# One transformer block, forward and backward: W1 and dW1 in blocks of two steps, with another order of pools and of the middle phase

## The chip, the cores and the metric

The kernel runs on one core of a Trainium2 chip. The metric is the time of one execution on the device, in microseconds (us). A core has a matrix engine (TensorE, PE in the profile), a vector engine (VectorE, DVE), a scalar engine (ScalarE, ACT), a general engine (GpSimd, POOL) and a queue engine that here only issues transfers (SyncE, SP). Each of them works through its own instructions in order. Transfers are issued from SP and from POOL and are carried out by 16 DMA engines. SBUF is the working memory with 128 partitions; PSUM holds the sums of matmuls.

## The reference

The kernel computes one block with adaptive layer norm, and all its gradients. Cut to its core:

```python
mod = (silu(c) @ w_mod).reshape(1, 6, 1, 512)       # sa, ca, ga, sb, cb, gb
h = layernorm(x) * (1 + ca) + sa
x = x + ga * attention(h, wqkv, wo)                 # 2048 tokens, 32 heads of 16, softmax
h = layernorm(x) * (1 + cb) + sb
u = h @ w1 + b1                                     # 512 -> 1792
x = x + gb * (relu(u) ** 2 @ w2 + b2)               # 1792 -> 512
# outputs: x, and the gradients of x, wqkv, wo, w1, b1, w2, b2, c, w_mod for a given grad_out
```

Inputs and outputs are bf16. For the change it matters that du, the gradient of u, is computed from grad_out; that dW1 is a product of the normalised x (xhat2) and du over all tokens, with two corrections that also need W1; and that dW2 is a product of relu(u)**2 and grad_out.

## The kernel before

The work is written out in one order, in the class `K`. `phase_fwd` runs forward attention head pair by head pair over four chunks of 512 tokens (`SC` = 4) and, between its steps, the qkv projections and the MLP with the first half of its backward part (`gen_mlp`) for chunks 0 to 2. `last_chunk` then does the MLP of chunk 3, for which there is no attention left to lie beside, and the weight gradients of the MLP. `phase5` is attention backward over 8 groups of four heads (`NQ`), two head pairs each, and `phase6` computes the rest. The order of TensorE and of SP is the program's own throughout; from attention backward on, POOL's is too. The order on VectorE and ScalarE (and on POOL before attention backward) is set by a planner, which keeps to program order where it can. Semaphores are set by the framework from what each tile is read and written by.

**The middle phase, `last_chunk`.** `bg` is what is left of chunk 2's MLP, `bg.take(n)` takes n units of it. For each of four blocks of 128 tokens the attention output is turned (`turn`, four transposes and a copy) and multiplied by wo (L800); x is added (L801), the layer norm's numbers are computed on VectorE and POOL (L802 to L806), and ScalarE writes the normalised block `xh` (L807). `xh` is turned to `xhT`. fc1 (L821) makes 14 tiles of relu(u) in `rT`; du (L794, the helper `du_mm`, which reads `gT`, the turned grad_out) makes 14 tiles that VectorE combines with `rT` to `duT` (L828). Three of the du tiles, `early[0]` to `early[2]`, are computed ahead: two inside the loop over blocks and one between the turns of `xh`; they lie in the PSUM pool `dps`, which has three banks. Then follow, for block k: `dx(k)` (L848, and the layer norm backward), `fc2(k)` (L879), `turn_dx(k)`, `do(k)` (L1237: the gradient of the attention output, its row sums, and the padded tile `dOpad`), and `turn_do(k)` (dOpad turned into `dOTq`, stored from SP by L874 after every second k). The order is written by hand:

```python
        fc2(2)
        turn_dx(2)
        fc2(3)
        turn_do(1)
        do(2)
```

**dW1 and dW2.** `fill` holds two generators. `gen_dw1` works in 14 steps of 128 columns of W1 (`FT`): 64 matmuls (L964) of `xh2` with the turned du block `du_blk` (a transposing load from `duT_d` on SP, L944, three buffers, issued two steps ahead), one small matmul with `diag` (L969), and then on ScalarE and VectorE the dW1 block and two dot products with the W1 block. One step has 16 units for `fill.take`. POOL loads the W1 block of each step (L947, three buffers of 128 columns), computes `diag` (L949) and stores the dW1 block (L985, two buffers). A block of 128 columns in bf16 is a run of 256 B in a row of W1 in memory. `gen_dw2` works in 14 steps of 16 matmuls (L1015) with `a_blk` (four buffers), then multiplies on VectorE (L1018), stores from POOL (L1019), and adds to a sum on POOL (L1022). The last such step is the last work ahead of attention backward.

**Pools.** SBUF is handed out as a stack from the left and one from the right. In the middle phase the left one holds, from below, e0 (x1, grad_out, xhat2), dw1 and dw2. They are closed at the end of `last_chunk`; `phase5` opens p56a (the gradients of q, k and v), p5pu (the exponentials `pu`, six buffers), p5kv, p5dt (`dsT`, four) and p5ds (`ds`, three), in this order, in the same place. A tile whose memory was held by a closed pool waits for those who used it.

**Attention backward.** For each head pair, each chunk of 512 keys and each group of four blocks of 128 queries: scores on TensorE (L1497), exponential on ScalarE (L1501), dP on TensorE (L1436), ds on VectorE (L1438), the key and value gradients (L1390), ds turned (a quarter by TensorE, L1455, copied by ScalarE, L1456; the rest by a transposing transfer on SP, L1446), and the query gradient (L1412). There are 256 such groups; each has eight exponentials and eight ds.

Of the kernel before, what the change touches and what calls it, by code (L numbers as in the profile page):

```python
# [9 lines left out]
BF16 = mybir.dt.bfloat16  # L10
F32 = mybir.dt.float32
# [8 lines left out]
P = 128  # L20
# [85 lines left out]
class K:  # L106
# [636 lines left out]
    def last_chunk(self, bg, O_b, x0s):  # L743
# [42 lines left out]
        ve = mk.tile([P, 4], F32, name="ve")  # L786
        rstd = mk.tile([P, 4], F32, name="rstd2")
        nmr = mk.tile([P, 4], F32, name="nmr")
        early = {}

        def du_mm(ft, pool, name):
            pt = pool.tile([P, 512], F32, name=name)
            for kt in range(DT):
                nc.tensor.matmul(pt[:], lhsT=self.W2gbT[:, ft, kt, :], rhs=gT[:, kt, :], start=(kt == 0), stop=(kt == DT - 1))  # L794
            return pt

        for k in range(4):
            pt = mps.tile([P, 512], F32, name="pps")
            for kt in range(DT):
                nc.tensor.matmul(pt[:], lhsT=OT[:, k, kt, :], rhs=self.wo[:, kt, :], start=(kt == 0), stop=(kt == DT - 1))  # L800
            nc.vector.tensor_tensor(x1[:, k, :], pt[:], x0s[k][:], ALU.add)  # L801
            nc.vector.bn_stats(stats[:, k, :], x1[:, k, :])  # L802
            nc.vector.bn_aggr(mv[:, k, :], stats[:, k, :])
            nc.vector.tensor_scalar(ve[:, k:k + 1], mv[:, k, 1:2], EPS, None, ALU.add)
            nc.gpsimd.tensor_tensor(rstd[:, k:k + 1], ve[:, k:k + 1], self.mhalf[:, k:k + 1], ALU.pow)
            nc.vector.scalar_tensor_tensor(nmr[:, k:k + 1], mv[:, k, 0:1], -1.0, rstd[:, k:k + 1], ALU.mult, ALU.mult)  # L806
            nc.scalar.activation(xh[:, k, :], x1[:, k, :], ACT.Identity, bias=nmr[:, k:k + 1], scale=rstd[:, k:k + 1])  # L807
            bg.take(1)
            if k > 1:
                early[k - 2] = du_mm(k - 2, self.dps, "dps")  # L810
        bg.drain()
        xhT = mk.tile([P, 4, DT, P], BF16, name="fT", bufs=2)
        for k in range(4):
            turn(xh[:, k, :], DT, xhT[:, k], "vector" if k % 2 else "scalar")
            if k == 2:
                early[2] = du_mm(2, self.dps, "dps")
        rT = self.rT_pool.tile([P, FT, 512], BF16, name="rT")
        for ft in range(FT):
            pt = mps.tile([P, 512], F32, name="pps")
# [4 lines left out]
        self.close_pool("mlp_u")  # L824
        duT = mk.tile([P, FT, 512], BF16, name="auT")
        for ft in range(FT):
            pt = early.get(ft) or du_mm(ft, mps, "pps")
            nc.vector.scalar_tensor_tensor(duT[:, ft, :], pt[:], 2.0, rT[:, ft, :], ALU.mult, ALU.mult,  # L828
                                           accum_out=self.db1_part[:, ft, sc:sc + 1])
            nc.scalar.activation(rT[:, ft, :], rT[:, ft, :], ACT.Square)  # L830
# [27 lines left out]
        def turn_dx(k):  # L858
            dxT = mk.tile([P, DT, P], BF16, name="dxT", bufs=2)
            turn(dxTs[k], DT, dxT[:], "scalar")  # L860
            dxTs[k] = dxT
# [5 lines left out]
        def turn_do(k):  # L867
            if k % 2 == 0:
                self.dOTq = mk.tile([P, NQ, 2 * P], BF16, name="dOTq")
            c0 = k % 2 * P  # L870
            turn(dOpads[k][:].rearrange("p g j e -> p (g j e)"), NQ, self.dOTq[:, :, c0:c0 + P], "scalar")
            if k % 2:
                t0 = (st0 + k - 1) * P
                nc.sync.dma_start(self.dOTq_d.rearrange("g p s -> p g s")[:, :, t0:t0 + 2 * P], self.dOTq[:])  # L874
# [20 lines left out]
        do(1)  # L895
        fc2(2)
        turn_dx(2)
        fc2(3)
        turn_do(1)
        do(2)  # L900
        self.close_pool("mlp_f")
        w2p = self.open_pool("dw2", bufs=2)
        g2 = self.gen_dw2(w2p, g_tm)
        fill.add(g2)
        fill.take(8)
        turn_dx(3)
        fill.take(8)
        turn_do(2)
        do(3)
        fill.take(24)  # L910
        turn_do(3)
        for name in ("mlp0", "mlpk"):
            self.close_pool(name)
# [13 lines left out]
    def gen_dw1(self, sb, xh2):  # L927
        nc, io = self.nc, self.io
        D, F, ST, DT, FT = self.D, self.F, self.ST, self.DT, self.FT
        db1 = self.db1  # L930
        w1_v = io["B_w1"].rearrange("(kt p) f -> p kt f", p=P)
        dw1_v = io["out_4"].rearrange("(kt p) f -> p kt f", p=P)
        dcb_part = sb.tile([P, DT, FT], F32, name="dcb_part", bufs=1)
        dsb_part = sb.tile([P, DT, FT], F32, name="dsb_part", bufs=1)
        db1_row = sb.tile([1, F], BF16, name="db1_row", bufs=1)
        nc.vector.memset(dcb_part[:], 0.0)
        nc.vector.memset(dsb_part[:], 0.0)
        blks = []

        def load(ft):  # L940
            r = sb.tile([P, ST, P], BF16, name="du_blk", bufs=3)
            cuts = (0, ST - 4, ST) if ft < 2 else (0, ST)
            for (a, b) in zip(cuts, cuts[1:]):
                nc.sync.dma_start_transpose(r[:, a:b, :], self.duT_d[ft, :, a * P:b * P])  # L944
            w = sb.tile([P, DT, P], BF16, name="w1_blk", bufs=3)
            with nc.allow_non_contiguous_dma(reason="256B runs"):
                nc.gpsimd.dma_start(w[:], w1_v[:, :, ft * P:(ft + 1) * P])  # L947
            diag = sb.tile([P, P], F32, name="diag", bufs=3)
            nc.gpsimd.tensor_scalar(diag[:], self.ident_f[:], db1[:, ft:ft + 1], 1.0, ALU.mult, ALU.mult)  # L949
            blks.append((r, w, diag))  # L950

        for ft in range(2):
            load(ft)
        yield 0
        for ft in range(FT):
            if ft + 2 < FT:
                load(ft + 2)
            else:
                yield ("dw1", 0)
            du, w1_blk, diag = blks[ft]  # L960
            g4 = self.dps.tile([P, DT, P], F32, name="dps")
            for kt in range(DT):
                for st in range(ST):
                    nc.tensor.matmul(g4[:, kt, :], lhsT=xh2[:, st, kt * P:(kt + 1) * P], rhs=du[:, st, :],  # L964
                                     start=(st == 0), stop=(st == ST - 1))
                    if st % 4 == 3:
                        yield 1
            csb_ps = self.mps.tile([P, 512], F32, name="pps")
            nc.tensor.matmul(csb_ps[:, :P], lhsT=self.ones_f[:], rhs=diag[:], start=True, stop=True)  # L969
            csb = sb.tile([P, P], F32, name="csb")  # L970
            nc.scalar.copy(csb[:], csb_ps[:, :P])
            nc.scalar.copy(db1_row[:, ft * P:(ft + 1) * P], csb_ps[0:1, :P])
            t1 = sb.tile([P, DT, P], F32, name="t1")
            dw1 = sb.tile([P, DT, P], BF16, name="dw1")
            for kt in range(DT):
                nc.scalar.activation(t1[:, kt, :], csb[:], ACT.Copy, scale=self.mod_col(3)[:, kt:kt + 1])
                nc.vector.scalar_tensor_tensor(dw1[:, kt, :], g4[:, kt, :], self.opcbT[:, kt:kt + 1], t1[:, kt, :], ALU.mult, ALU.add)
                junk = sb.tile([P, P], F32, name="junk")
                nc.vector.scalar_tensor_tensor(junk[:], g4[:, kt, :], 1.0, w1_blk[:, kt, :], ALU.mult, ALU.mult,
                                               accum_out=dcb_part[:, kt, ft:ft + 1])  # L980
                junk2 = sb.tile([P, P], F32, name="junk")
                nc.vector.scalar_tensor_tensor(junk2[:], csb[:], 1.0, w1_blk[:, kt, :], ALU.mult, ALU.mult,
                                               accum_out=dsb_part[:, kt, ft:ft + 1])
            with nc.allow_non_contiguous_dma(reason="256B runs"):
                nc.gpsimd.dma_start(dw1_v[:, :, ft * P:(ft + 1) * P], dw1[:])  # L985
        nc.gpsimd.dma_start(io["out_5"].rearrange("(o f) -> o f", o=1), db1_row[:])
        nc.vector.tensor_reduce(self.dcb_col[:], dcb_part[:], axis=AX.X, op=ALU.add)
        nc.vector.tensor_reduce(self.dsb_col[:], dsb_part[:], axis=AX.X, op=ALU.add)
# [286 lines left out]
    def phase5(self):  # L1275
        S, D, NQ, ST, DT = self.S, self.D, self.NQ, self.ST, self.DT
        nc, io = self.nc, self.io
        opa = self.open_pool("p56a", bufs=1)
        self.pup = self.open_pool("p5pu", bufs=6)
        self.dq_t = opa.tile([P, ST, D], BF16, name="dq_t")  # L1280
        self.dk_t = opa.tile([P, ST, D], BF16, name="dk_t")
# [8 lines left out]
        self.parts = [self.dq_t, self.dk_t, self.dv_t]  # L1290
        self.stp = self.open_pool("p5st", bufs=3, space=PSUM)
        self.dpp = self.open_pool("p5dp", bufs=3, space=PSUM)
        self.kvp = self.open_pool("p5kv", bufs=1)
        self.dtp = self.open_pool("p5dt", bufs=4)
        self.dsp = self.open_pool("p5ds", bufs=3)
        self.accp = self.open_pool("p5acc", bufs=1, space=PSUM)
        self.attn_bwd()

# [273 lines left out]
    def phase6(self):  # L1572
# [5 lines left out]
        tc, nc, pp, io = self.tc, self.nc, self.pp, self.io  # L1578
        S, D, H, ST, DT = self.S, self.D, self.H, self.ST, self.DT
        NT = 3 * DT  # L1580
        for name in ("p5ds", "p5dt", "p5kv", "p5pu", "p5q", "p5c", "p5acc"):
            self.close_pool(name)
        sb = self.open_pool("p6", bufs=1)
        wk = self.open_pool("p6w", bufs=1, side="right")
# [275 lines left out]
```

## Time and profile before

Three runs took 2565.96, 2576.85 and 2575.13 us.

| | |
|---|---|
| median of the runs | 2575.13 us |
| profiled execution | 2565.96 us |
| its span, first to last instruction | 2564.2 us |
| mean granted clock of TensorE | 0.995 |
| busy: TensorE, ScalarE, VectorE, POOL | 2464.7, 2313.3, 1762.0, 559.6 us |
| middle phase without attention beside it | about 980 to 1164 us of the span |
| attention backward | about 1164 to 2435 us |

Times in the text are us from the start of the span. In a row of the order of time, the first number is the start, the second the length (of a group of instructions: from the first start to the last end), then engine, line, operation, the tiles written and read, the count, and in brackets how long the engine stood idle before it and what ended that. In a row of waits, the engine and line that waited stand left, what ended the wait right, with the total, the number and the longest.

### The profile page before, as it was taken

What the parts mean: (1) busy time and instruction counts of PE and PEld (TensorE: products, weight loads), DVE (VectorE), ACT (ScalarE), POOL (GpSimd) and SP (SyncE); (2) the same over time, 40 slices, a digit from 0 to 9 for tenths busy, and PEclk for the clock granted to TensorE, in tenths of its full rate; (3) what the DMA queues carried; (4) which work ended last, traced back from release to release, by engine and by line L of the source; (5) the groups of instructions that cost most, each with busy time, mean ns of one, the idle gap of its engine ahead of it and who ended that gap; (6) DMA issues with size and microseconds to landing.
All of it is one profiled execution on the core that took longest, in us unless ns stands there. A gap on an engine that the chain in (4) does not pass through costs nothing.

```text
span 2564.2 us, 77585 instructions
## 1 busy us (share of the span) xinstructions
PE 2464.7 (96%) x31011; PEld 1222.2 (48%) x31239; DVE 1762.0 (69%) x3651; ACT 2313.3 (90%) x3761; POOL 559.6 (22%) x1113
## 2 busy tenths in 40 slices
PE   8999899999999998999999999999999999999997
PEld 4555555555555554763444444444444444444443
DVE  6222223423322344668999999999999999999876
ACT  7999999999999996417999999999999999999854
POOL 3454521310221131452111111111111111101122
PEclk9999999999999999999999999999999999999998
DMA  4588652440452144999999999999999999999996
GB/s 165 117 180 197 175 92 90 110 105 22 121 128 48 48 137 116 250 222 210 201 199 202 201 200 201 194 206 203 199 199 201 200 207 198 198 199 205 225 213 156
DMA packets 1196032, 432.18 MB, mean 169 GB/s; under 512 B 1137604, under 2 KB 1163078, under 8 KB 1195670
## 3 DMA queue, kind: packets, MB, share of 16 engines
q1 hardware_dynamic: 1158342, 324.75, 65.1%
q0 software_dynamic: 37328, 102.47, 13.5%
q8 instruction: 244, 4.00, 0.6%
q14 instruction: 118, 0.97, 0.1%
HBM read 74.26 MB, written 68.69 MB: 56 GB/s over the span
## 4 chain that ended last, share of the span: by engine, by line
PE 60%; ACT 29%; issue 5%; DMA 4%; DVE 1%; POOL 0%; SPq 0%; ACTq 0%; DVEq 0%; POOLq 0%
ACT pu L385 25%; PE st L1497 19%; PE acckv L1390 10%; PE accq L1412 8%; PE st L382 4%; PE dp L1436 3%; ACT pu L1501 2%; PE st L1455 2%; PE dps L1015 2%; PE accbank L316 2%; DMA dsT<-ds 2%; PE dp L1546 1%; PE dps L964 1%; PE st L1638 1%; PE pps L1176 1%
## 5 line engine op out<-in xcount | busy, mean ns | idle before, releaser
L1438 DVE TENSOR_TENSOR ds<-dp,pu 128x512 bf16<-128x512 f32 x2048 | 1236.7, 681 | 17.7 <-PE dp L1436 11.1
L1501 ACT ACTIVATE pu<-st 128x512 bf16<-128x512 f32 x2048 | 1074.1, 612 | 76.5 <-PE st L1497 50.7
L385 ACT ACTIVATE pu<-st 128x1024 bf16<-128x1024 f32 x992 | 911.9, 1077 | 3.9 <-PE st L382 3.5
L382 PE MATMUL st<-QTm,KTq 128*128 128x512 bf16 x1859 | 560.6, 377 | 26.9 <-ACT pu L385 6.0
L316 PEld LDWEIGHTS <-pu 128*128 128x128 bf16 x8192 | 346.8, 96 | 235.7 <-issue 2.3
L316 PE MATMUL accbank<-Vaug,pu 128*128 128x17 bf16 x8192 | 357.5, 171 | 8.3 <-ACT Vaug L505 1.1
L1436 PE MATMUL dp<-m,q 64*128 64x512 bf16 x1024 | 345.2, 382 | 4.9 <-DVE ds L1438 4.1
L1436 PE MATMUL dp<-m,dOTg 64*128 64x512 bf16 x1024 | 344.4, 381 | 0.0
L1412 PEld LDWEIGHTS <-dsT 128*128 128x128 bf16 x8192 | 239.8, 96 | 213.6 <-issue 209.4
L1497 PE MATMUL st<-m,QTg 64*128 64x512 bf16 x1024 | 319.0, 381 | 9.7 <-ACT pu L1501 8.0
L1497 PE MATMUL st<-m,q 64*128 64x512 bf16 x1024 | 319.5, 382 | 9.1 <-ACT pu L1501 7.5
L382 PEld LDWEIGHTS <-KTq 128*128 128x128 bf16 x1984 | 188.3, 96 | 176.6 <-issue 124.9
L1485 POOL COPY tick<-ds 1x1 bf16<-1x1 bf16 x215 | 37.9, 176 | 1019.7 <-DVE ds L1438 1019.7
L1456 ACT COPY dsT<-st 128x512 bf16<-128x512 bf16 x256 | 152.5, 596 | 5.0 <-PE st L1455 5.0
L1390 PE MATMUL acckv<-ds,Qg 128*16 128x512 bf16 x1024 | 154.1, 381 | 0.0
L1390 PE MATMUL acckv<-pu,dOg 128*16 128x512 bf16 x1024 | 154.1, 381 | 0.0
L1390 PE MATMUL acckv<-pu,q 128*16 128x512 bf16 x1024 | 154.0, 381 | 0.0
L1390 PE MATMUL acckv<-ds,q 128*16 128x512 bf16 x1024 | 154.0, 381 | 0.0
L1412 PE MATMUL accq<-q,dsT 128*128 128x16 bf16 x4096 | 144.3, 170 | 1.6 <-DMA dsT<-ds 1.6
L1412 PE MATMUL accq<-Kg,dsT 128*128 128x16 bf16 x4096 | 143.2, 170 | 2.0 <-DMA dsT<-ds 2.0
L296 POOL DMA_DIRECT2D QTm<-QTq_d x124 | 63.1, 511 | 335.5 <-PE st L382 314.8
L323 DVE RECIPROCAL rl<-accbank 128x4 f32<-128x4 f32 x128 | 22.9, 179 | 151.5 <-PE accbank L316 151.4
(363 smaller groups left out, 2798.6 us busy)
## 6 DMA issues: line engine op xcount, KB each, us to landing
KTq<-KTq_d POOLq DMA_DIRECT2D x24, 512.0 KB, 3.8
duT_d<-auT POOLq DMA_DIRECT2D x4, 1792.0 KB, 8.8
aT_d<-rT POOLq DMA_DIRECT2D x3, 1792.0 KB, 12.5
KTq_d<-KTq SPq DMA_DIRECT2D x32, 128.0 KB, 1.8
QTq_d<-ev_fm SPq DMA_DIRECT2D x32, 128.0 KB, 2.9
VTq_d<-vT POOLq DMA_DIRECT2D x4, 1024.0 KB, 6.4
O_d<-O POOLq DMA_DIRECT2D x4, 1024.0 KB, 5.5
dsT<-ds SPq DMA_TRANSPOSE x256, 6.6
```

The costliest lines, as they stand in the source:

```text
L296: nc.gpsimd.dma_start(QTm[j][32 * j:32 * j + 32, :], self.QTq_d[g, 32 * j:32 * j + 32, 512 * qc:512 * (qc + 1)])
L316: nc.tensor.matmul(acc[:, a, sub, :], lhsT=pu[:, a, sub * P:(sub + 1) * P], rhs=Vaug[:, kb, h, :], start=(kb == 0 and a == 0 and sub == 0) ...
L382: nc.tensor.matmul(stt[:, a, :], lhsT=KT[:, kb * P:(kb + 1) * P], rhs=QTm[2 * jp + a][:], start=True, stop=True)
L385: nc.scalar.activation(pu[:], stt[:], ACT.Exp, scale=self.scale)
L1015: nc.tensor.matmul(pt[:], lhsT=a[:, st, :], rhs=g_tm[:, st, :], start=(st == 0), stop=(st == ST - 1))
L1390: nc.tensor.matmul(acckv[r:r + DH, :], lhsT=T[n][:, ib, col:col + DH], rhs=src[:, a, :], start=(ib == 0), stop=(ib == ST - 1))
L1412: nc.tensor.matmul(accq[:, ib, a, :], lhsT=dsT[:, (i * 2 + a) * 4 + sub, :], rhs=T["K"][:, 4 * c + sub, col:col + DH], start=(c == 0 and i ...
L1436: nc.tensor.matmul(dp[:], lhsT=T["dOT"][rd, ib * P:(ib + 1) * P], rhs=masked["VT"][2 * jp + a][rd, 512 * c:512 * (c + 1)], start=True, sto ...
L1438: nc.vector.tensor_tensor(dsg[:, i, a], dp[:], pu[:, a, :], ALU.mult)
L1456: nc.scalar.copy(dsT[:, 0:4, :], tp[:])
L1497: nc.tensor.matmul(stt[:], lhsT=T["QT"][rs, q], rhs=masked["KT"][2 * jp + a][rs, c0:c0 + 512], start=True, stop=True)
L1501: nc.scalar.activation(pu[:, a, :], stt[:], ACT.Exp, scale=self.scale)
```

## The change

The change has four parts.

1. `gen_dw1` loads W1 for two steps at once (128 x 4 x 256 elements, two buffers), so that the runs in memory are 512 B, and uses one half of the tile in each step; dW1 is collected in a tile of the same shape and stored after every second step.
2. `du_mm` and the three early du tiles go; all 14 du tiles are computed in one loop behind fc1, in the PSUM pool of the other products.
3. `turn_do(1)` moves ahead of `fc2(3)`, and the units of dW1 between the last steps are 4, 4 and 32 where they were 8, 8 and 24.
4. `phase5` opens its pools in another order: p56a, p5ds, p5pu, p5dt, p5kv. `phase6` closes them in the matching order.

```diff
-        early = {}
-
-        def du_mm(ft, pool, name):
-            pt = pool.tile([P, 512], F32, name=name)
-            for kt in range(DT):
-                nc.tensor.matmul(pt[:], lhsT=self.W2gbT[:, ft, kt, :], rhs=gT[:, kt, :], start=(kt == 0), stop=(kt == DT - 1))
-            return pt
-
         for k in range(4):
...
             bg.take(1)
-            if k > 1:
-                early[k - 2] = du_mm(k - 2, self.dps, "dps")
         bg.drain()
...
             turn(xh[:, k, :], DT, xhT[:, k], "vector" if k % 2 else "scalar")
-            if k == 2:
-                early[2] = du_mm(2, self.dps, "dps")
...
         for ft in range(FT):
-            pt = early.get(ft) or du_mm(ft, mps, "pps")
+            pt = mps.tile([P, 512], F32, name="pps")
+            for kt in range(DT):
+                nc.tensor.matmul(pt[:], lhsT=self.W2gbT[:, ft, kt, :], rhs=gT[:, kt, :], start=(kt == 0), stop=(kt == DT - 1))
...
         turn_dx(2)
+        turn_do(1)
         fc2(3)
-        turn_do(1)
         do(2)
...
-        fill.take(8)
+        fill.take(4)
         turn_dx(3)
-        fill.take(8)
+        fill.take(4)
         turn_do(2)
         do(3)
-        fill.take(24)
+        fill.take(32)
         turn_do(3)
...
-            w = sb.tile([P, DT, P], BF16, name="w1_blk", bufs=3)
-            with nc.allow_non_contiguous_dma(reason="256B runs"):
-                nc.gpsimd.dma_start(w[:], w1_v[:, :, ft * P:(ft + 1) * P])
+            if ft % 2 == 0:
+                w2 = sb.tile([P, DT, 2 * P], BF16, name="w1_blk", bufs=2)
+                nc.gpsimd.dma_start(w2[:], w1_v[:, :, ft * P:(ft + 2) * P])
+                ws.append(w2)
+            w = ws[-1][:, :, ft % 2 * P:(ft % 2 + 1) * P]
...
-            dw1 = sb.tile([P, DT, P], BF16, name="dw1")
+            if ft % 2 == 0:
+                dw1_2 = sb.tile([P, DT, 2 * P], BF16, name="dw1")
+            dw1 = dw1_2[:, :, ft % 2 * P:(ft % 2 + 1) * P]
...
-            with nc.allow_non_contiguous_dma(reason="256B runs"):
-                nc.gpsimd.dma_start(dw1_v[:, :, ft * P:(ft + 1) * P], dw1[:])
+            if ft % 2:
+                nc.gpsimd.dma_start(dw1_v[:, :, (ft - 1) * P:(ft + 1) * P], dw1_2[:])
...
         opa = self.open_pool("p56a", bufs=1)
+        self.dsp = self.open_pool("p5ds", bufs=3)
         self.pup = self.open_pool("p5pu", bufs=6)
...
+        self.dtp = self.open_pool("p5dt", bufs=4)
         self.kvp = self.open_pool("p5kv", bufs=1)
-        self.dtp = self.open_pool("p5dt", bufs=4)
-        self.dsp = self.open_pool("p5ds", bufs=3)
```

More of the change, by code (lines that the diff above doesn't have):

```diff
@@ L937, in gen_dw1 @@
         nc.vector.memset(dsb_part[:], 0.0)
-        blks = []
+        blks, ws = [], []
         def load(ft):
@@ L1580, in phase6 @@
         NT = 3 * DT
-        for name in ("p5ds", "p5dt", "p5kv", "p5pu", "p5q", "p5c", "p5acc"):
+        for name in ("p5kv", "p5dt", "p5pu", "p5ds", "p5q", "p5c", "p5acc"):
             self.close_pool(name)
```

## The prediction

> **What bounds the kernel now.** I read the page first, then the waits of TensorE over the one stage that the diff touches (980 to 1175 us of the span; forward attention ends there, backward attention begins), then stretches of that stage, then the order of time on each engine. The page says that TensorE is busy nearly always; the chain of the whole execution is mostly exponentials, matmuls and little else.
>
> ```profile
> span 2564.2 us, 77585 instructions
> ...
> PE 2464.7 (96%) x31011; PEld 1222.2 (48%) x31239; DVE 1762.0 (69%) x3651; ACT 2313.3 (90%) x3761; POOL 559.6 (22%) x1113
> ```
>
> In the stage itself the waits of TensorE (who waited on which line, for what, us in total, times, longest) are few, and the first three of these lines hold nearly all that an edit here could win back:
>
> ```profile
> PE dps L794 <- DMA fT<-in_grad_out_dram: 4.1, 1, 4.1
> PE dp L1436 <- DVE ds L1438: 4.1, 1, 4.1
> PE dps L964 <- DMA du_blk<-duT_d: 1.3, 2, 1.1
> ...
> PE dps L964 <- DVE junk L982: 0.2, 1, 0.2
> ```
>
> The first is an early du tile standing in TensorE's queue until gT has landed. The second is the start of backward attention: the first ds waits for the store of the last dW2 block. VectorE's waits name that store:
>
> ```profile
> DVE dw L977 <- DMA out_dram<-dw: 4.2, 4, 2.3
> ...
> DVE ds L1438 <- DMA out_dram<-dw: 3.8, 1, 3.8
> ```
>
> In the order of time of single engines (start, length, engine, line; in brackets the idle time before and what ended it), from which all times below are taken, the two places read:
>
> ```profile
> 992.76 1.49 PE L794 MATMUL dps<-fT,W2gbT 128*128 128x512 bf16 x4 [4.14 <-DMA fT<-in_grad_out_dram]
> 994.04 1.91 PE L800 MATMUL pps<-wo,fT 128*128 128x512 bf16 x4
> ...
> 1164.40 3.05 ACT L1501 ACTIVATE pu<-st 128x512 bf16<-128x512 f32 x6 [50.65 <-PE st L1497]
> ...
> 1165.03 0.57 POOL L1019 DMA_DIRECT2D out_dram<-dw  x1
> ...
> 1169.74 30.80 DVE L1438 TENSOR_TENSOR ds<-dp,pu 128x512 bf16<-128x512 f32 x51 [3.83 <-DMA out_dram<-dw]
> ```
>
> The stretches (start:end, length, busy us by engine, granted clock, DMA share, GB/s) show that from 1002.5 to 1163.9 us TensorE sets the pace, and that its clock falls after a long idle time:
>
> ```profile
> 988.60:992.70 4.10, 0.02 (x1) 0.00 (x0) 2.67 (x12) 1.63 (x2) 1.66 (x3) 1.00 0.99 167
> 992.70:994.50 1.80, 1.74 (x6) 0.68 (x6) 0.00 (x0) 0.00 (x0) 0.00 (x0) 0.63 0.95 291
> 994.50:996.00 1.50, 1.50 (x5) 0.57 (x4) 0.01 (x1) 0.00 (x0) 0.00 (x0) 0.50 0.97 313
> ...
> 1014.60:1024.10 9.50, 9.45 (x45) 4.31 (x45) 6.80 (x19) 6.36 (x11) 0.00 (x0) 1.00 0.00 1
> ...
> 1069.30:1111.90 42.60, 42.41 (x726) 42.12 (x727) 36.68 (x224) 17.33 (x66) 19.63 (x30) 1.00 1.08 227
> 1111.90:1163.90 52.00, 51.74 (x238) 23.50 (x243) 22.05 (x59) 1.59 (x6) 33.70 (x42) 1.00 1.05 232
> ...
> 1170.50:1172.50 2.00, 2.00 (x11) 0.80 (x11) 1.94 (x4) 0.81 (x2) 0.00 (x0) 0.50 0.00 0
> ```
>
> The profiled execution took 2565.96 us (span 2564.2, 1.8 around it), 9.2 us under the median of the three runs, 2575.13. The sum is made against 2565.96 and the same difference is put on the median. The three runs lie 10.9 us apart, so about 0.5% (13 us) is what a measurement can tell from no change.
>
> **Early du tiles removed.** Before, TensorE stands 4.14 us (988.62 to 992.76) in front of the first early tile, with the fourth output-projection block behind it; that block runs at 994.04, its layer-norm ends on ScalarE at 998.66 + 0.81 = 999.47, and fc1 starts at 1002.50. Without the early tiles the fourth block waits only for its PSUM bank, which VectorE frees with the read of the third (989.32 + 0.68 = 990.0). Four matmuls at 0.215 and their drain: 991.1. VectorE is free at 991.87; from there the chain of before (add at 995.99, xhat done at 999.47) takes 3.48: 995.35. Then two copies on ScalarE (0.59 each) with four transposes (0.23) between, and the small gaps, about 2.0: fc1 at 997.4, 5.1 earlier. The 12 matmuls of the three tiles return behind fc1, where TensorE is packed: 12 x 0.2155 = 2.6. Net -2.5. Between 993.4 and 997.4 TensorE has only 16 transposes. After 4.1 us of idle time the rows show a clock of 0.63 and 0.50 until about 996.5; after 1.14 us (1063.46 to 1064.60) the next matmuls kept their full rate. If fc1 starts at half rate for 3.4 us, some 8 matmuls of 0.215 are lost, 1.7. I count half of that: -1.7, with ends of -3.3 (the chain a little shorter, full clock) and +1.7 (the chain gains only the 2.6 that returns, half clock).
>
> The Trainium skill, TensorE: Matmul & The Clock Gate, section Part 1, has the array fall to half rate after an idle window of about 3.4 us and return after a busy one of that length. The rows agree for the 4.1 us stall. By the rule alone no whole window before fc1 would be idle, fc1 would start at full rate, and the term would be -2.5.
>
> **Order of the pools of backward attention.** Sizes per partition from the code, in KB from the bottom of the left stack: e0 ends at 42; pool dw1 at 78.4 before, 81.4 after (w1_blk 4 for 3, dw1 4 for 2); pool dw2 is 29 long. p56a ends at 50.05. Before, pu takes 50 to 62 and lies over dw1 alone, which is done at 1116; so the first exponential runs at 1164.40 without a wait and six run ahead; ds takes 98 to 122 and meets dw2, so it waits for the last store (issued 1165.03, 4.43 long, landed at 1169.46). After, ds takes 50 to 74 over dw1 alone: its wait of 3.83 goes. But pu takes 74 to 86 and dw2 begins at 81.4. What is late next is then the first exponential. In the compiled program of before the first dsT copy, whose own bytes lie over dw1 only but whose pool reaches into dw2, carries waits for dw2's last stores: waits go by pool. So I take it that the exponential waits for that store, on ScalarE, with every later exponential and the dsT copies behind it: first exponential at 1169.5, first ds after its 0.55 at 1170.2, 0.45 later than 1169.74. The lead is gone too: before, seven score and three dp matmuls were done in the wait, now three and one. The clock then is 0.50 (row above), matmuls start 0.43 apart (1171.54, 1171.94, 1172.37), four of a unit are 1.72, against 1.21 for its two ds (51 in 30.80 us). Two such units until the clock is back: 1.0. Sum +1.5; ends: -3.8 (waits go by bytes; a_blk's readers are matmuls already past), +3 (half clock throughout its 6.8 us). From 1180 on each group takes the same as before: eight ds of 0.604 are 4.83 of a period of 4.87 to 4.89, so a later start is carried to the end and nothing is won back.
>
> **Order of turn_do(1) and the fills.** All 40 units of dW1 still lie before turn_do(3), so TensorE's work is equal; its cover isn't. In the times of before: turn_do(1) now comes at 1049.55, but VectorE writes the last pad of dOpad 1 at 1050.66 + 0.20: 1.35 idle, with fc2(3), do(2) and all else queued behind. do(2) ends at 1055.6 for 1054.12. Then 4 units (0.9), turn_dx(3) (0.23), 4 units: 1057.6. dOpad 2 was done 3.34 after do(2) (1057.46); so now at 1058.9: 1.35 idle again. Together +2.7. On SP's queue the first dOTq store stands ahead of the du_blk transposes and waits for ScalarE's copy of turn_do(1); it moves about 2 earlier, so the third du_blk lands near 1062.6 for 1064.60, and the waits of 1.14 and 0.17 go: -1.3. The fourth du_blk waits for the first dW1 step's last matmul, now at 1062.6 for 1059.6, and lands 8.5 later (1060.70 to 1069.23 before), just when it is needed: +0.3. ScalarE's wait of 3.8 for the dOTq store shrinks; nothing of TensorE hung on it. Net +1.7; ends -1.3 (VectorE takes the pads first and nothing waits) and +4 (both waits longer by one 0.68 operation, transposes later).
>
> **Pairs of blocks.** Seven loads and seven stores fewer, 14 x 0.75 of POOL's issue time, which is no bound (19.6 of 42.6). A dW1 buffer is now free two steps later than needed, so VectorE's 4.2 of waits for stores go; TensorE saw 0.2 of them (VectorE is busy 36.7 of 42.6, three PSUM banks between). The pair load waits for the same VectorE step as before, then has two steps, 7.7, to land; singles land in 4.4. The first pair stands ahead of duT's store on POOL as two singles stood around it. -0.2; ends -0.4, +1 (a pair that lands late).
>
> ```profile
> DMA packets 35615, 12.89 MB, mean 226 GB/s; under 512 B 33616, under 2 KB 34664, under 8 KB 35604
> ...
> q0 software_dynamic: 1436, 3.86, 21.9%
> ```
>
> In 1060 to 1117 the queue of these loads and stores moved 3.86 MB in 1436 packets, 2.7 KB each, so its packets aren't the 256 B runs; the small packets are the transposes' queue.
>
> The Trainium skill, DMA: Bandwidth & Descriptors, section Specifications, wants at least 512 B per transfer for line rate. By it each load and store would be much quicker; the most that this could give TensorE is the same 0.2.
>
> **Sum:** -1.7 + 1.5 + 1.7 - 0.2 = +1.3: 2567.3 in an execution like the profiled one, 2576.4 on the median.
>
> **Rivals.**
> - Waits by bytes: the ds wait goes and no other comes. -1.7 - 3.8 + 1.7 - 0.2 = -4.0, 2571. For it: ds waited where it overlaps the stored tile. Against it: the dsT copy above.
> - Slower: without its lead ScalarE (152 busy of 156 us per stretch) settles into another order against VectorE (154 of 156). It decides from 50 ns per group: 256 x 0.05 = +12.8, 2589. For it: both are full, so any swap shows. Against it: the lead is bounded by the same six buffers, and the period was equal in eight stretches.
> - The pairs free the DMA engines (share 1.08 in the dW1 step) and the transposes land earlier everywhere: at best the du_blk waits and half of the stalls of turn_do, -1.3 more, on top of waits by bytes: 2570. Against it: packets are large already.
>
> **How the numbers follow.** Forecast 0.55, waits by bytes 0.20, slower period 0.17, freed DMA 0.08. Terms between their ends give -5 to +10 around the median; runs themselves spread 9 below and 2 above. Range 2563 to 2590 leaves out the far part of the slower rival and the lowest runs of the quick ones. By cases (faster, same, slower): forecast 0.02, 0.48, 0.05; bytes 0.03, 0.17, 0; period 0, 0.07, 0.10; DMA 0.03, 0.05, 0. Together 0.08, 0.77, 0.15.
>
> **What would show it.** TensorE's 4.1 for gT gone and fc1 near 997; a ScalarE wait of about 5 before the first exponential, for the dW2 store, and none at ds; TensorE idle at turn_do(1) and turn_do(2), over 1 us each; no wait of dW1's first step for stores; the same group period. Wrong if the exponential starts at 1164, if fc1 doesn't move, or if stretches after 1180 hold fewer ds.

## The result, and the profile after

The changed kernel took 2609.34 us (median of four runs, 2604.12 to 2614.28) against 2571.47 (four runs, 2565.96 to 2576.85) of the kernel before: a ratio of 1.0147, with a 95% interval of 1.0114 to 1.018. It is about 38 us slower, and outside the range of 2563 to 2590 that was forecast. The profiled execution took 2607.56 us.

The page of the kernel after, its span and busy times:

```profile
span 2605.8 us, 77540 instructions
...
PE 2471.3 (95%) x31011; PEld 1223.9 (47%) x31239; DVE 1766.5 (68%) x3651; ACT 2317.0 (89%) x3761; POOL 549.0 (21%) x1099
```

No engine has much more to do than before: TensorE 6.6 us, VectorE 4.5, ScalarE 3.7. The 41.6 us that the span has grown are waits. Three points in time divide them, the first ds, the last ds and the end:

| | before | after | difference |
|---|---|---|---|
| first ds starts | 1169.7 | 1174.7 | +5.0 |
| from there to the start of the last ds | 1257.7 | 1289.1 | +31.4 |
| from there to the end | 136.8 | 142.0 | +5.2 |

So three quarters lie in attention backward, in the stretch in which the prediction had every group take the same as before. Stretches of the middle of it (start:end, length, busy us of TensorE, weight loads, VectorE, ScalarE, POOL with counts, granted clock, DMA share, GB/s), first the kernel before:

```profile
1336.00:1492.00 156.00, 153.60 (x2188) 65.99 (x2180) 154.43 (x257) 152.11 (x303) 19.48 (x56) 1.00 1.01 202
1648.00:1804.00 156.00, 153.60 (x2189) 66.05 (x2186) 154.90 (x258) 152.37 (x302) 18.97 (x55) 1.00 1.02 201
```

and the kernel after:

```profile
1336.00:1492.00 156.00, 150.06 (x2146) 64.76 (x2145) 151.41 (x252) 149.23 (x296) 18.76 (x54) 1.00 1.21 196
1648.00:1804.00 156.00, 149.31 (x2138) 64.45 (x2136) 150.58 (x250) 148.34 (x294) 18.76 (x54) 1.00 1.19 197
```

The last three columns give it away. TensorE's clock is full in both. The DMA engines are busy for 1.2 in place of 1.0 of the stretch (the share adds up the times of all packets, and so can pass 1) and yet move less, 196 GB/s and not 202: a packet takes longer in the mean. VectorE, ScalarE and TensorE all lose 3 to 4 us of 156 together, which is what engines do that wait for the same thing. What the thing is, the chain that ended last says for 1336 to 2272 us of the kernel after:

```profile
by line: DMA dsT<-ds 40.4%; PE st L1491 23.3%; PE acckv L1384 12.9%; PE accq L1406 10.8%; ACT pu L1495 3.5%; issue 2.5%; PE dp L1430 2.5%; PE st L1449 2.1%; PE st L1395 1.3%; ACT kvT L1387 0.6%; ACT dv_t L1399 0.3%; ACT dk_t L1399 0.0%
```

In the kernel before the same entry was 1.9%. It is the transposing transfer of ds, one per group. The answer on the tile dsT gives, for the transfer, the time that its issue takes on SP's queue (the row with SPq: ns, smallest, median, largest), the time for which TensorE's weight loads and matmuls stood waiting for it, and the time from issue to landing. Before:

```profile
L1446 SPq DMA_TRANSPOSE dsT<-ds x256: 3397/3619/5714, 1174.8 to 2429.1; - x128
...
  DMA dsT<-ds: 7.7, 10
...
DMA to landing us min/median/max: 5.2/6.6/9.3
```

After:

```profile
L1440 SPq DMA_TRANSPOSE dsT<-ds x256: 4167/4835/8757, 1180.1 to 2470.0; - x128
...
  DMA dsT<-ds: 85.2, 121
...
DMA to landing us min/median/max: 6.4/8.2/11.2
```

The median issue grew from 3.62 to 4.84 us, in a loop whose period was 4.91 (1257.7 / 256): SP's queue, which had a quarter of its time to spare, is all but full (4.84 of a new period of 5.04, 1289.1 / 256). Over 1336 to 2272 us these transfers held the queue for 719.9 of 936 us before and for 884.5 after, and the pause between two of them fell from 1.2 to 0.09 us (medians). The diff touches neither this transfer nor its size. The engines' own work on ds did not get longer: one ds takes VectorE 681 ns in both kernels, a weight load from ds 96, and a matmul with it 381 before and 382 after.

In the middle phase the waits of TensorE after (980 to 1180 us) are those that the prediction named, the one for du_blk, which it had let go, and one more at the turns ahead of fc1; the 4.1 us for gT are gone:

```profile
PE st L1491 <- ACT pu L1495: 4.3, 1, 4.3
PE tp L763 <- DVE dOpad L1257: 3.1, 2, 1.8
PE dps L956 <- DMA du_blk<-duT_d: 2.4, 3, 0.9
PE tp L763 <- ACT fT L764: 2.0, 1, 2.0
PE pps L792 <- DVE x_l L793: 1.4, 1, 1.4
```

and the places in the order of time, on TensorE, ScalarE and VectorE:

```profile
989.92 1.02 PE L792 MATMUL pps<-wo,fT 128*128 128x512 bf16 x4 [1.43 <-DVE x_l L793]
...
997.11 13.35 PE L809 MATMUL pps<-fT,w 128*128 128x512 bf16 x56 [0.52 <-DVE fT L764]
...
1049.61 0.61 PE L763 MATMUL tp<-ident,dOpad 128*128 128x128 bf16 x8 [1.79 <-DVE dOpad L1257]
1050.05 4.87 PE L869 MATMUL pps<-w,rT 128*128 128x512 bf16 x14
...
1059.53 0.61 PE L763 MATMUL tp<-ident,dOpad 128*128 128x128 bf16 x8 [1.31 <-DVE dOpad L1257]
...
1174.05 3.04 ACT L1495 ACTIVATE pu<-st 128x512 bf16<-128x512 f32 x6 [55.67 <-DMA out_dram<-dw]
...
1174.67 2.63 DVE L1432 TENSOR_TENSOR ds<-dp,pu 128x512 bf16<-128x512 f32 x4 [4.13 <-ACT pu L1495]
```

### The profile page after: what moved, and what is told of

It reads as the page before. It is cut to its first block, busy times and chain, and to the rows that moved or that the text cites. A ratio compares the mean times of both kernels' runs of the same rounds, so it can differ in the third digit from the quotient of the medians.

```text
span 2605.8 us, 77540 instructions
## 1 busy us (share of the span) xinstructions
PE 2471.3 (95%) x31011; PEld 1223.9 (47%) x31239; DVE 1766.5 (68%) x3651; ACT 2317.0 (89%) x3761; POOL 549.0 (21%) x1099
## 4 chain that ended last, share of the span: by engine, by line
PE 30%; DMA 23%; ACT 2%; issue 2%; DVE 1%; POOL 0%; ACTq 0%; POOLq 0%; DVEq 0%
DMA dsT<-ds 21%; PE st L1491 12%; PE acckv L1384 6%; PE accq L1406 5%; PE dps L1009 2%; ACT pu L1495 2%; PE dp L1430 1%; PE dps L956 1%; PE st L1449 1%; DMA du_blk<-duT_d 1%; DMA out_dram<-dwm 1%; PE st L1395 1%; PE gps L1675 0%; DVE junk L1560 0%; DMA out_dram<-dx 0%
## 5 line engine op out<-in xcount | busy, mean ns | idle before, releaser
L1406 PEld LDWEIGHTS <-dsT 128*128 128x128 bf16 x8192 | 245.1, 96 | 256.4 <-issue 208.7
L1430 PE MATMUL dp<-m,dOTg 64*128 64x512 bf16 x1024 | 338.6, 382 | 0.0
L1406 PE MATMUL accq<-Kg,dsT 128*128 128x16 bf16 x4096 | 150.2, 171 | 23.8 <-DMA dsT<-ds 22.9
```

The costliest lines, as they stand in the source:

```text
L1406: nc.tensor.matmul(accq[:, ib, a, :], lhsT=dsT[:, (i * 2 + a) * 4 + sub, :], rhs=T["K"][:, 4 * c + sub, col:col + DH], start=(c == 0 and i ...
L1430: nc.tensor.matmul(dp[:], lhsT=T["dOT"][rd, ib * P:(ib + 1) * P], rhs=masked["VT"][2 * jp + a][rd, 512 * c:512 * (c + 1)], start=True, sto ...
```

## The experiments

**The theory.** Part 4 of the change doesn't only alter what waits for what. It also moves the tiles to other addresses. p56a ends at 78.219 KB in each partition, which is 224 B past a multiple of 256 B. (These are the addresses that the program assigns; the prediction counted from the bottom of the left stack, 28.156 KB lower.) Before, the pools that follow end with ds at 126.25 KB and dsT at 94.25 KB, both on multiples of 256 B, because p5kv holds, beside kvT, a tile named `tick` that takes 32 B, and 224 + 32 = 256. After, the pool with `tick` comes last: ds lies at 78.219 KB and dsT at 114.219 KB, both 224 B past a multiple. Each has buffers of 8 KB, so all buffers of a tile share its offset. The transposing transfer reads ds and writes dsT in pieces of 256 B (681517 of the 687597 packets from 1336 to 2272 us before; the others have 4 B).

**The rivals.** First, the prediction's own: without the six exponentials that ran ahead, ScalarE and VectorE settle into another, longer order. Second, the order of the pools costs by another way, a wait or a shared buffer. Third, the middle phase costs it.

### The same change with the address put right, and the kernel before with it put wrong

Both runs have one edit, a longer `dsa_part` in p56a (and its two uses, written to match); the 32 B more are never read. One is made in the kernel after, where it brings ds and dsT back to multiples of 256 B; the other in the kernel before, where it takes both 32 B off.

```diff
-        self.dsa_part = opa.tile([P, DT, 3], F32, name="dsa_part")
+        self.dsa_part = opa.tile([P, DT * 3 + 8], F32, name="dsa_part")[:, 0:DT * 3].rearrange("p (a b) -> p a b", b=3)
...
```

> The changed kernel with one tile of p56a (dsa_part) 32 B longer, so that ds, pu and dsT begin 32 B higher and ds and dsT fall on multiples of 256 B; the order of the pools and all else stays. Theory A (the transposing transfers of ds to dsT are slower where their two tiles begin 32 B off): a dsT transfer lands in 6.6 us as in the kernel before and not in 8.2, the period of a group falls from 5.07 to 4.89 us, and 256 x 0.15 to 0.18 = 38 to 46 us, less some 5 that the middle phase lost, come back: the time is 2570 to 2580. Theory B (the order of the pools: the exponentials start without a lead and the two engines settle into a worse order): the start is the same as in the changed kernel, so nothing comes back: 2605 to 2613.

> The kernel before with the same tile 32 B longer: ds, dsT and kvT begin 32 B off a multiple of 256 B, nothing else changes. Theory A: dsT transfers land in about 8 us, the period is about 5.05, the time is 2605 to 2615. Theory B: nothing changes, 2566 to 2577.

Measured, beside 2572.05 us of the kernel before (median of 19): the change with the address put right 2572.18 us (ten executions), a ratio of 0.9999 (0.9988 to 1.001); the kernel before with it put wrong 2607.55 us (four), 1.014 (1.0118 to 1.0163). The answer on dsT, of the first:

```profile
L1440 SPq DMA_TRANSPOSE dsT<-ds x256: 3396/3618/7691, 1178.6 to 2431.4; - x128
...
DMA to landing us min/median/max: 5.5/6.8/8.6
```

and of the second:

```profile
L1446 SPq DMA_TRANSPOSE dsT<-ds x256: 4168/4859/7016, 1177.4 to 2467.0; - x128
...
DMA to landing us min/median/max: 6.4/8.1/10.5
```

The 32 B decide all of it, in both directions, and the rest of the change comes to nothing that the times can tell. The first rival falls: the lead of six exponentials is missing from the first of these kernels and present in the second. The third falls as well.

### The side that is read, or the side that is written

Pads at the start of the pools, in the kernel before. The first moves ds alone by 32 B. The second moves dsT by 32 B and takes ds on to the next multiple of 256 B.

```diff
         self.dsp = self.open_pool("p5ds", bufs=3)
+        nc.gpsimd.memset(self.dsp.tile([P, 16], BF16, name="pad_s", bufs=1)[:], 0.0)
```

```diff
         self.dtp = self.open_pool("p5dt", bufs=4)
+        nc.gpsimd.memset(self.dtp.tile([P, 16], BF16, name="pad_t", bufs=1)[:], 0.0)
         self.dsp = self.open_pool("p5ds", bufs=3)
+        nc.gpsimd.memset(self.dsp.tile([P, 112], BF16, name="pad_s", bufs=1)[:], 0.0)
```

> The kernel before with 32 B ahead of ds in its pool: only ds, the side that the transposing transfers read, is 32 B off. If the reading side costs, 2600 or more; if the writing side costs, 2566 to 2580; if both share it, between, near 2590. Theory B: 2566 to 2580.

> The kernel before with 32 B ahead of dsT and ds put back on a multiple of 256 B: only dsT, the side that the transposing transfers write, is 32 B off. If the writing side costs, 2600 or more; if the reading side costs, 2566 to 2580; if both share it, near 2590. Theory B: 2566 to 2580.

ds alone off: 2604.24 us (two executions), 1.0126 (1.0094 to 1.0158), landing after 8.3 us. dsT alone off: 2575.51 us (eight), 1.002 (0.999 to 1.005), landing after 6.8 us. So it is the side that is read.

### How far off, and whether 512 B is better still

The same pad at the start of p5ds in the kernel before, of 64, 128 and 256 B (`[P, 32]`, `[P, 64]`, `[P, 128]` in bf16). Before, ds lies on an odd multiple of 256 B; the last of these puts it on a multiple of 512 B.

> The kernel before with ds alone moved 64 B up from its multiple of 256 B (a pad of 64 B ahead of it); dsT and everything else keep their places. If what counts is that a block of 64 B begins on a multiple of 64, nothing happens: 2572 us within 0.3%, dsT transposes issued in 3.62 us and landing after 6.8. If whole multiples of 128 or 256 B are needed, it is as with 32 B off: about 2604 us, issue 4.85 us, landing 8.2. If the loss grows with the distance from the multiple, it is worse than at 32 B, above 2610.

> The kernel before with ds alone moved 128 B up. If multiples of 64 or of 128 B suffice: 2572 us within 0.3%, issue 3.62 us, landing 6.8. If each row of 256 B must begin on a multiple of 256 B: about 2604 us, issue 4.85 us, landing 8.2. Beside the run with 64 B off this gives the step.

> The kernel before with ds moved 256 B up: from an odd multiple of 256 B to a multiple of 512 B. If 256 B is the unit that counts, a row of 256 B touches one unit in both: 2572 us, issue 3.62 us, landing 6.6 to 6.8. If the unit is 512 B or more, the transposes get faster still: issue under 3.5 us, and the wait of the queue falls; the time itself would then move little, since VectorE's ds alone takes 1236.7 us of the 1257.7 between the first and the last ds: 2560 at best.

64 B off: 2615.89 us, 1.0145 (1.0073 to 1.0217). 128 B off: 2610.41 us, 1.0123 (1.0062 to 1.0184). On a multiple of 512 B: 2574.59 us (ten executions), 0.9996 (0.9975 to 1.0017). The first two ran only twice each, 2605.33 and 2626.44 us, 2604.20 and 2616.62, beside 2573.80 of the kernel before (median of 19; by the medians alone the ratios would be 1.0163 and 1.0142), so their times alone, which lie above the 2610 of the third case foreseen, do not tell a flat price from a growing one. Their transfers do. In the order of the three runs:

```profile
L1447 SPq DMA_TRANSPOSE dsT<-ds x256: 4200/4834/7349, 1187.2 to 2475.5; - x128
```

```profile
L1447 SPq DMA_TRANSPOSE dsT<-ds x256: 4174/4831/7171, 1182.1 to 2466.8; - x128
```

```profile
L1447 SPq DMA_TRANSPOSE dsT<-ds x256: 3422/3643/5828, 1179.2 to 2435.0; - x128
```

A multiple of 256 B is the unit: 64 and 128 B off cost the same as 32, and 512 B gains nothing. The price on the transfer is flat, not one that grows with the distance; in the profile of 64 B off, the 2626.44 us, the time beyond that lies outside the stretch from the first ds to the last: 156.9 us from dx's start to the first, 152.5 behind the last, for 145.6 and 136.8 in the kernel before.

The view of the transfers over 1336 to 2272 us gives the mean time of one packet of SP's queue, as its share times 16 engines times 936 us over its packets. In the kernel before and in the kernel after it reads:

```profile
q1 hardware_dynamic: 687597, 174.49, 98.0%
```

```profile
q1 hardware_dynamic: 673892, 171.01, 114.3%
```

0.980 x 16 x 936000 / 687597 = 21.3 ns, and 25.4 ns after. For all runs of this kind, with the offset of ds from a multiple of 256 B and the time from the first to the last ds:

| kernel | ds off by | packet, mean | first to last ds |
|---|---|---|---|
| before | 0 | 21.3 ns | 1257.7 us |
| after, address put right | 0 | 21.3 | 1257.5 |
| before, dsT alone off | 0 | 21.5 | 1257.2 |
| before, on a multiple of 512 B | 0 | 21.6 | 1259.1 |
| before, 32 B (both tiles) | 32 | 25.4 | 1291.7 |
| before, 32 B (ds alone) | 32 | 25.5 | 1286.8 |
| before, 64 B | 64 | 25.4 | 1290.1 |
| before, 128 B | 128 | 25.7 | 1286.6 |
| after | 224 | 25.4 | 1289.1 |

About 4 ns a packet in the mean at every offset. The single packets show that it is not 4 ns on each: of those of 256 B, 97.4% take 18 ns or less before and 87.5% still do after, as in the other runs off a multiple (87.7 to 88.6%). The additional time lies in a minority of longer ones, 2.5 of the 4 ns in packets of 100 ns and more (0.57% of them before, 1.07% after). Over the nine runs of the study with ds on a multiple the stage takes 1256.4 to 1260.0 us, over the five without 1286.6 to 1291.7; the means differ by 30.6 us, 0.119 us for each of the 256 groups. The offset decides; whether SP's queue or the DMA engines behind it set the new period, no run separates.

The Trainium skill has a rule for this: DMA: Bandwidth & Descriptors, section How a descriptor splits into AXI transactions, says that every transaction of a transfer has to begin on a multiple of 256 B; by it a piece of 256 B that doesn't begin there needs two transactions in place of one. The boundary agrees with these runs: 0 and 256 B are quick, 32, 64, 128 and 224 are not. The mean time does not follow the page's beats of 32 B: as an estimate by its rule, 256 B cost 8 beats aligned and, for these four offsets, 9, 10, 12 and 15, where the runs show 25.4 to 25.7 ns for all four. Why most packets keep their 18 ns and a few take much longer stays open. And no run shows a price on the written side.

### The parts one by one

Five more kernels hold one or two parts of the change each, in the kernel before, with ds and dsT on multiples of 256 B. Each ran eight or ten times, beside 2573.80 us of the kernel before (early tiles, order of fills) or 2574.48 (the others). The order of pools alone (with the longer `dsa_part`, and `phase6` closing them in the matching order):

```diff
         opa = self.open_pool("p56a", bufs=1)
+        self.dsp = self.open_pool("p5ds", bufs=3)
         self.pup = self.open_pool("p5pu", bufs=6)
...
-        self.kvp = self.open_pool("p5kv", bufs=1)
         self.dtp = self.open_pool("p5dt", bufs=4)
-        self.dsp = self.open_pool("p5ds", bufs=3)
+        self.kvp = self.open_pool("p5kv", bufs=1)
```

> The kernel before with the pools of the backward attention in the order of the kernel after (ds, pu, dt, kv), and dsa_part 32 B longer so that ds and dsT stay on multiples of 256 B; nothing else. By the prediction's second step the wait of the first dp for ds goes, the first exponential waits for the last store of dW2, and it costs 1.5 us up to the first ds; the stage from first to last ds stays at 1257 to 1260 us, and the time at 2572 to 2576. Rival: the order of the pools itself, not the address, is what costs 30 us: then 2600 and more.

2573.61 us, 0.9996 (0.9973 to 1.0019), and 1258.8 us from first to last ds. The second rival falls. ScalarE's first exponential and VectorE's first ds in the order of time:

```profile
1175.85 3.04 ACT L1501 ACTIVATE pu<-st 128x512 bf16<-128x512 f32 x6 [58.90 <-DMA out_dram<-dw]
...
1176.48 2.63 DVE L1438 TENSOR_TENSOR ds<-dp,pu 128x512 bf16<-128x512 f32 x4 [6.56 <-ACT pu L1501]
```

The wait has moved from ds to the exponential, as the prediction had it. The early du tiles alone taken out:

```diff
-            pt = early.get(ft) or du_mm(ft, mps, "pps")
+            pt = mps.tile([P, 512], F32, name="pps")
+            for kt in range(DT):
+                nc.tensor.matmul(pt[:], lhsT=self.W2gbT[:, ft, kt, :], rhs=gT[:, kt, :], start=(kt == 0), stop=(kt == DT - 1))
```

(and `early` and `du_mm` with it)

> The kernel before without its three early du tiles, nothing else changed; ds and dsT keep their multiples of 256 B. By the prediction's first step fc1 starts at 997.4 us in place of 1002.50, loses about 0.85 us to a clock that has dropped, and du takes 2.6 us more, so that the dx matmuls start 1.7 us earlier than 1024.10: at 1022.4, and the span is 1.7 us shorter, 2562.5. Rival: the dx matmuls wait for something else of that stage, and start at 1024.1 as before.

2577.25 us, 1.0003 (0.9977 to 1.0028). In the order of time on TensorE:

```profile
996.42 13.36 PE L809 MATMUL pps<-fT,w 128*128 128x512 bf16 x56 [0.52 <-DVE fT L764]
1009.62 12.25 PE L817 MATMUL pps<-fT,W2gbT 128*128 128x512 bf16 x56
1021.70 3.62 PE L838 MATMUL pps<-W1mT,auT 128*128 128x512 bf16 x16
```

dx starts at 1021.7. The start of this stage itself differs between executions by up to 3 us, so it is better measured from the last MLP matmul of the chunks before (L1166 here): 80.5 us. In the four kernels without early tiles it is 80.5 to 80.6; in the ten with them 79.9 to 83.1, median 82.1. That is 1.5 us won by the median; one of the ten, the one with the pairs alone, is quicker even so. The time shows none of it. The order of the fills alone:

```diff
+        turn_do(1)
         fc2(3)
-        turn_do(1)
         do(2)
...
-        fill.take(8)
+        fill.take(4)
         turn_dx(3)
-        fill.take(8)
+        fill.take(4)
...
-        fill.take(24)
+        fill.take(32)
```

> The kernel before with the second turn of dO ahead of fc2(3) and the fillers in parts of 4, 4 and 32, nothing else changed; addresses as before. By the prediction's third step: two stalls of 1.35 us, 1.3 us won back since du_blk is there earlier, 0.3 us more: +1.7, so that the backward attention's first st matmul starts at 1165.5 in place of 1163.85. By the profile of the changed kernel: the stalls are 1.8 and 1.3 us, nothing is won back, and fc2(3) is 1.7 us longer at a dropped clock: +4.5 to +5, first st matmul at 1168.5, span about 2569.

2577.59 us, 1.0002 (0.9977 to 1.0026). TensorE's order of time:

```profile
1052.63 0.61 PE L763 MATMUL tp<-ident,dOpad 128*128 128x128 bf16 x8 [1.47 <-DVE dOpad L1263]
1053.08 3.19 PE L879 MATMUL pps<-w,rT 128*128 128x512 bf16 x14
...
1060.87 0.61 PE L763 MATMUL tp<-ident,dOpad 128*128 128x128 bf16 x8 [1.31 <-DVE dOpad L1263]
```

The two stalls are there, 1.47 and 1.31 us, but fc2(3) takes 3.19 us and not the 4.87 of the kernel after. Its waits for du_blk are 3.9 us in total: nothing is won back there. The first score matmul of attention backward came at 1171.70, later than both times expected (1165.5 and 1168.5); in the seven kernels with the code of before (before itself and the six that only move tiles) it comes at 1163.85 to 1176.56. Nor does a wait for dOpad belong to the new order alone: in three executions with the old one TensorE waits 2.0 to 4.0 us for it. The pairs alone, and the pairs with the early tiles taken out (their edits are those of the change):

> The kernel before with W1 loaded and dW1 stored in pairs, nothing else changed, ds and dsT in their places. By the prediction's fourth step it gives 0.2 us: 2572 to 2574 us; VectorE waits for no store of dW1, and the time from the first csb to the first ds is 108 us as before (1061.7 to 1169.7). Rival: the pairs double what a step waits for, loads of 256 KB land later than 128 KB did, and the csb chain is some us longer than in the kernel before.

> The kernel before with pairs and without the early du tiles; pools, order of fills and addresses as before: the parts that by the prediction's steps gain something, 1.7 and 0.2 us. Expected 2571 us against 2573, which a comparison of the times can hardly tell from none; the dx matmuls start at 1022, and the first ds comes at 1168 if the gain is passed on, at 1170 or later if a wait for du_blk takes it.

The pairs alone took 2582.35 us, 1.0033 (1.0012 to 1.0055), a little slower; with the early tiles taken out 2575.29 us, 1.0001 (0.9977 to 1.0024). In its profile the kernel with the pairs alone starts the last ds 1256.4 us after the first, like all aligned ones. As expected, VectorE waits for no store of dW1 in it; from its first `csb` (a copy in the first dW1 step) to the first ds it takes 110.1 us, within the 108.0 to 115.5 of the kernels with the code of before, so the rival of a longer chain isn't seen. It waits longer than before for the turned du block:

```profile
PE dps L966 <- DMA du_blk<-duT_d: 4.8, 2, 3.5
```

This answer does not settle it: the kernel with pairs and without early tiles waits 4.8 there too and took no longer than before, and the whole change with the address put right, which has the pairs, is at 0.9999. Whether the pairs by themselves cost 8 us, or these runs came out long, stays open.

Lastly, what the middle phase can show at all. From dx's start to the first ds, seven kernels run the code of before (before itself, the one with both tiles off, and those with pads): 145.6 to 156.9 us, median 149.1; the profile that the prediction was made from is the shortest of the seven. With parts of the change, or all of it, it takes 149.4 to 154.2: nothing there separates from before. The waits for du_blk differ likewise, from 1.3 us in the first profile to 4.3 in another with the same code in this phase.

No version here beats the kernel before: the fastest ratios, 0.9996, are no different from one.

## Why the prediction was wrong

**The step that failed** is the end of the order of pools: "From 1180 on each group takes the same as before: eight ds of 0.604 are 4.83 of a period of 4.87 to 4.89, so a later start is carried to the end and nothing is won back." The group takes 0.119 us more, 30.6 us over 256 groups, because the order of the pools put ds 32 B short of a multiple of 256 B. The prediction's own sign came with it: stretches of 156 us after 1180 hold 250 to 252 operations of VectorE and not 257 or 258. The period was read rightly as VectorE's, but with three others right behind it: ScalarE with 152 of 156 us in a stretch, the DMA engines with a share of 1.0, and SP's queue with 3.62 us of 4.91. A price on the transfer alone, 1.2 us of issue, was enough to pass VectorE. The prediction had worked out where the pools come to lie, to 0.1 KB, to see what they overlap, and did not ask what the last 32 B do to a transfer that reads them; the skill's rule quoted above speaks against this change and was not weighed. The loss of 38 us by the medians is larger than 30.6; the interval of the ratio, 1.0114 to 1.018, is 29 to 46 us and holds it. The 10 us that the two profiles differ outside this stage lie within what the seven kernels with the code of before show there: the first ds at 1174.7 us after, against 1169.7 to 1182.1, and 142.0 us behind the last, against 136.8 to 152.5.

**The slower rival** had the place and the size (decides from 50 ns a group; it was 119) and the wrong cause, ScalarE's order, so that its nearness to the result is luck. The run with the address put right has the same order without the lead, and the same period as before.

**Early du tiles, -1.7:** right in its mechanism and near in size, 1.5 by the medians. fc1 started at 997.11 for 997.4 forecast, dx at 1022.39 for 1022.4; that dx came so near is luck, since the four kernels without these tiles start it at 1021.70 to 1023.81. fc1 took 13.35 us for 12.26 before, a loss of 1.1 where half of 1.7 was put.

**First exponential, +1.5:** right in its mechanism (ScalarE waits for dW2's last store; ds then 0.62 behind it). Its size lies within the spread of the phase: the first ds came at 1174.7 after and 1173.2 with the address put right, both inside the 1169.7 to 1182.1 above. Waits by bytes, the first rival, is refuted by the same row.

**Order of turn_do(1), +1.7:** the stalls came, 1.79 and 1.31 for 1.35 twice; the -1.3 for an earlier du_blk did not, since its waits in the profile after are 2.4 us; and fc2(3) was 1.7 longer in that one execution. None of it is seen in the times.

**Pairs, -0.2:** VectorE's 4.2 us of waits for stores of dW1 are gone, as forecast, in all four kernels with pairs. No gain is seen in the times; see above for what stays open. The third rival, freed DMA engines, is not borne out: in the dW1 steps their share is 1.06 after for 1.08 before, within the 1.03 to 1.13 of the seven kernels with the code of before, and the waits for du_blk and dOpad are still there. The stretch in the kernel after:

```profile
1069.30:1111.90 42.60, 40.10 (x680) 39.28 (x678) 34.18 (x218) 16.80 (x61) 11.40 (x19) 1.00 1.06 211
```

**What the sum was made of.** All its terms were of 1 to 2 us, read from one execution, in a phase which in executions of the same code takes 145.6 to 156.9 us. With the address put right the sum of +1.3 is not contradicted, nor told from nothing: 0.9999 (0.9988 to 1.001) is -3 to +3 us.

## What to carry to other kernels

When a pool is moved, work out the address of each tile in it to the byte, and see whether a tile that a transposing transfer reads in pieces of 256 B begins on a multiple of 256 B; here a small tile ahead of it decided. A loop in which several engines and queues are nearly full should be examined for each of them, the issue queue included: here a transfer that was not the period became it by 1.2 us. Here a higher DMA share with fewer GB/s in the same stretch said that packets had become longer in the mean, and pointed at the transfer and not at the order of the work.

## What was not expected of the hardware

- A transposing transfer from SBUF to SBUF whose source rows begin off a multiple of 256 B took 25.4 to 25.7 ns per packet in the mean and not 21.3 to 21.6, with 87.5 to 88.6% of the packets still at 18 ns or less; its issue held SP's queue for 4.84 us and not 3.62. The offset itself, 32, 64, 128 or 224 B, made no difference, and the written side, 32 B off, none either.
- The length of an idle time alone did not decide whether TensorE's clock fell. In the profile after, 1.79 us of waiting ahead of turn_do(1) were followed by a granted clock of 0.64 over the next 3.4 us, and fc2(3) took 4.87 us; after 1.47 and 1.54 us at the same place in two other runs it took 3.19. In the kernel with the pairs alone, 2.44 us of waiting ahead of turn_do(1) were followed by a full clock. These executions give no threshold.

The stretches around these places, first of the kernel after, then of the kernel with the pairs alone:

```profile
1047.80:1049.60 1.80, 0.01 (x1) 0.03 (x1) 1.62 (x8) 0.58 (x1) 1.80 (x4) 1.00 0.80 270
1049.60:1053.00 3.40, 3.40 (x17) 1.55 (x18) 0.00 (x0) 1.01 (x1) 0.22 (x1) 0.64 1.33 277
```

```profile
1051.30:1053.75 2.45, 0.02 (x1) 0.02 (x1) 1.31 (x7) 0.00 (x0) 2.42 (x5) 1.00 0.22 51
1053.75:1057.00 3.25, 3.24 (x47) 2.78 (x48) 0.31 (x1) 1.01 (x1) 0.22 (x1) 1.00 1.14 336
```
